# New costs and a new table of rank shifts in the planner of a fused recurrent-attention and gated-MLP kernel

## The chip, the core and the metric

The kernel runs on one core of a Trainium2 chip. The metric is the device time of one execution in microseconds (us); lower is better. TensorE (PE) multiplies matrices, VectorE (DVE), ScalarE (ACT) and GpSimd (POOL) do elementwise work, SyncE (SP) issues most DMA transfers. Every engine takes its own instructions strictly in program order, so an instruction that waits holds back all those behind it on its engine.

## The reference

Batch B is 4, heads H 8, sequence S 768, head dimension D 48; the model width is 384 and the inner width 1024. First a linear-attention recurrence runs over time for each batch and head, then a position-wise network with a short convolution in its gate:

```
for t in range(S):
    cur = u * k[t] (outer) v[t]
    y[t] = r[t] @ (state + cur)
    state = w[t][:, None] * state + k[t] (outer) v[t]
x = y, heads side by side                       # (4, 768, 384)
h = relu(x @ w_in)                              # 384 -> 1024
conv = sum over j of conv_w[j] * h shifted by j - 1 in time
out = (h * sigmoid(conv)) @ w_out               # 1024 -> 384
```

The weights arrive as 64-bit floats.

## The kernel before

The recurrence is cut into 24 chunks of 128 time steps, six to a batch (chunk n here; the stages in the planner are l, a and b). For each chunk: stage l loads w, k, r and v (line 602, four transfers of 192 KB each, small pieces); stage a transposes them on PE (637, after a small copy on ACT, 631), scans the decays on DVE (646, 654), multiplies (652, 658), transposes the keys back (705, copied out by ACT at 707 and 708), forms a diagonal on POOL (684, 686, 697) and sends a few rows to other partitions with six transfers (680, tile `last`); stage b does the score, state and output products on PE (846, 856, 878, 888) and writes x as a high and a low part (ACT 938, DVE 940), with six more transfers `xT<-xT` (949) after the fourth and the sixth chunk of a batch. The first four chunks have a longer form of stage b and no transfers of `last` (672 and 765 to 817). w, k and r have two buffers each, v three: chunk n + 2 can't be loaded before chunk n has released its buffer.

The network runs in 8 blocks of 384 time steps, two to a batch. A block is 8 units of nine matmuls of 386 columns each (960) into one PSUM bank, followed for each unit by the gate: ACT relu (972) and mul (973), two DVE steps (974, 976), ACT sigmoid (978), DVE product (979), ACT cast (981) and POOL difference (982), which makes the tile `gh`. Then 72 matmuls (989) per block multiply `gh` with w_out, three output tiles with 24 each, and ACT copies each out (1020) for SP to send (1021).

The weights are turned from 64-bit floats into a high and a low part during the first 70 us: three gathers of w_in issued by POOL (562), three transfers of w_out issued by SP (573), two of 1152 KB and one of 768 KB, and 17 pieces that go through ACT 513, DVE 515 and 518, POOL 521, ACT 535 and POOL 536. They share a ring of five large buffers with `gh`.

Which instruction comes when is decided by a planner at build time (class Plan). Each operation is recorded with an engine, a length from the table LEN, its dependencies, its buffers and a rank. `issue` then plays the engines forward with these lengths and always takes, of the operations that are ready on a free engine, the one with the lowest rank. The rank is the one the code gives plus two entries of the table SHIFT, one for the stage (a13, i2, l15 and so on) and one for the kind of operation in that sort of stage. The order that comes out is the program order of each engine; nothing is reordered on the chip. The places that matter:

```
def op(self, eng, us, f, r=(), w=(), holds=(), moves=0.0, port=False, rank=None):
...
        us = LEN[us] if isinstance(us, str) else us
...
        self.ops.append((eng, us, f, deps, bufs, moves, port,
                         (self.rank if rank is None else rank) + sum(SHIFT.get(x, 0) for x in self.tags[i]) + i * 1e-6))
```

Of the kernel before, what the change touches and what calls it, by code (L numbers as in the profile page):

```python
# [36 lines left out]

LEN = dict(
    tr=0.245, kback=0.245, scores=1.0, carried=0.794, state=0.45, y=0.86, state_y=1.22, mm3=0.529,
    cross=0.33, half=1.0, output=0.8, cph=0.35, sa=0.27, xhih=0.28, xloh=0.33,  # L40
    scan=0.86, small=0.1, pad=0.07, kt=0.47, dg=0.47, cp=0.62, xlo=0.6, sd=0.22, s=0.27,
    stt=0.54, gate=0.47, wts=0.47, wstt=0.47,
    fill=0.19, kh=0.37, guard=0.62, sbd=0.34, xhi=0.49, relu=0.41, mul=0.47, sig=0.43, cast=0.41, out=0.37, exp=0.46,
    z=0.98, zh=0.67, diag=1.07, lo=0.97,
    words=1.15, top=0.1, sdl=0.27, fetch=1.5, gather=1.6, rest=0.3, carried_rows=1.4, y_rows=1.5, ones=0.8,
    load=0.55, issue=0.45, spread=0.64,
)
SHAPE = dict(cross=3, half=3, output=3, scores=1, state=2, y=2, state_y=2, y_rows=2)
TURN = dict(tr=0.18, kback=0.18, carried=0.18)
PAUSE = 0.08  # L50
SHIFT = dict(
    a0=-1896, a1=-1164, a10=286, a11=83, a12=-1897, a13=911, a14=35, a15=-171, a16=-838, a17=1023, a18=300, a19=955,
    a2=-817, a20=586, a21=-198, a22=-206, a23=274, a3=1466, a4=-3102, a5=-229, a6=-1026, a7=10, a8=212, a9=-563,
    adg=1282, adiag=276, afill=1499, agather=13, aguard=-7, akback=213, akh=813, akt=-868, aones=389, apad=-30,
    ascan=-787, asmall=-226, aspread=-2165, atop=477, atr=208, az=393, azh=62, b1=1079, b10=-169, b12=280, b13=120,
    b15=457, b16=28, b17=396, b18=-3, b19=-2, b2=2308, b20=-53, b21=-561, b22=-32, b24=13, b3=1200, b4=735, b5=2,
    b6=-84, b7=-77, b8=111, b9=-911, bcarried_rows=234, bcp=20, bcph=432, bcross=-1208, bfill=93, bhalf=162, bkh=-259,
    boutput=-276, brest=97, bs=-396, bsa=-6, bscores=-136, bsd=-3, bsdl=-159, bsmall=-4, bspread=-44, bstate=56,
    bxhih=-258, bxloh=-167, by_rows=933, c=78, cexp=1328, cfill=595, cissue=24, clo=526, ctr=-113, cwords=-477,
    cwstt=94, cwts=43, i0=-1329, i1=-383, i2=266, i3=74, i4=-98, i7=-238, icast=-264, imm3=926, imul=12, irelu=-1875,  # L60
    isig=721, istt=-303, k=-7, kissue=22, ksmall=-75, l0=-32, l10=-37, l11=-2104, l12=3, l13=-294, l14=300, l15=702,
    l16=-1411, l17=589, l18=-103, l19=-154, l20=-57, l21=-30, l22=54, l23=-124, l3=-48, l4=95, l5=357, l6=82, l7=225,
    l8=668, l9=-175, lload=14, o0=-546, o1=-325, o2=210, o3=240, o4=-602, o6=60, o7=92, oissue=-254, omm3=1526,
    oout=-16, p0=-96, p1=-579, p10=77, p11=-444, p12=-378, p14=174, p15=52, p16=103, p2=-959, p3=-916, p4=17, p5=124,
    p6=357, p7=-445, p8=-626, p9=241, pcast=14, pexp=155, plo=-119, pwstt=100, pwts=107, q0=-465, q1=-346, q2=379,
    q3=-62, q4=91, q5=614, qissue=-23, qwords=31, w2=-1, w3=534, w5=112, w6=-73, wfetch=34, wissue=584,
)
TAIL = dict(PE=0.22, DVE=0.11, ACT=0.13, POOL=0.07, SP=2.3, LOAD=1.8)
BEGIN = dict(PE=4.3, DVE=3.0, ACT=3.2, POOL=8.3, SP=0.8)
# [1108 lines left out]
```

## Time and profile before

| what | value |
| --- | --- |
| median of 3 runs | 345.59 us (345.53, 345.59, 347.17) |
| the profiled execution | 346.11 us |
| its span, first to last instruction | 344.5 us |
| PE busy | 324.0 us, 94% of the span |
| DVE, ACT, POOL busy | 257.5, 228.4, 184.7 us |
| granted TensorE clock over the span | 0.98 |

The span is what the trace shows; 1.6 us of the profiled execution lie around it. A busy PE is not a PE at its peak, since matmuls overlap, and a granted clock under 1.00 in a stretch means that part of it ran at the lower of TensorE's two levels (1.2 GHz where 2.4 GHz is full).

### The profile page before, as it was taken

What the parts mean: (1) busy time and instruction counts of PE and PEld (TensorE: products, weight loads), DVE (VectorE), ACT (ScalarE), POOL (GpSimd) and SP (SyncE); (2) the same over time, 40 slices, a digit from 0 to 9 for tenths busy, and PEclk for the clock granted to TensorE, in tenths of its full rate; (3) what the DMA queues carried; (4) which work ended last, traced back from release to release, by engine and by line L of the source; (5) the groups of instructions that cost most, each with busy time, mean ns of one, the idle gap of its engine ahead of it and who ended that gap; (6) DMA issues with size and microseconds to landing.
All of it is one profiled execution on the core that took longest, in us unless ns stands there. A gap on an engine that the chain in (4) does not pass through costs nothing.

```text
span 344.5 us, 11004 instructions
## 1 busy us (share of the span) xinstructions
PE 324.0 (94%) x4278; PEld 302.1 (88%) x4278; DVE 257.5 (75%) x600; ACT 228.4 (66%) x610; POOL 184.7 (54%) x243
## 2 busy tenths in 40 slices
PE   8888886999999999899999999999999999999993
PEld 3877875889999989798999999999998999999992
DVE  4797999999999997679898788979575546786000
ACT  4276786897767652765868577565778998887201
POOL 8987999997376671244863185238122324444200
PEclk9989899999999999899999999999999999999998
DMA  8999945443456556366434533455747720000102
GB/s 155 278 307 324 231 94 102 90 80 79 85 122 134 105 119 129 71 139 122 107 65 108 123 84 69 94 107 126 242 133 211 233 66 25 24 0 26 50 23 73
DMA packets 114177, 40.95 MB, mean 119 GB/s; under 512 B 103021, under 2 KB 110726, under 8 KB 113350
## 3 DMA queue, kind: packets, MB, share of 16 engines
q1 hardware_dynamic: 112180, 30.74, 40.0%
q10 hardware_dynamic: 1506, 6.29, 5.9%
q0 software_dynamic: 432, 3.15, 2.2%
q8 instruction: 35, 0.57, 0.7%
q14 instruction: 24, 0.20, 0.2%
HBM read 31.48 MB, written 4.72 MB: 105 GB/s over the span
## 4 chain that ended last, share of the span: by engine, by line
PE 53%; POOL 11%; DMA 11%; DVE 8%; ACT 6%; SPq 5%; issue 4%; DVEq 0%; POOLq 0%; ACTq 0%
PE bank L989 21%; PE bank L960 20%; SPq L680 4%; PE bank L637 3%; DMA v<-in_v_dram 3%; DMA r<-in_r_dram 3%; POOL wide L521 2%; PE bank L846 2%; DMA gh<-in_moe_w_in_dram,limits 2%; DVE a L974 2%; PE bank L856 2%; POOL pm L697 2%; DVE g L979 1%; DVE a L976 1%; PE bank L878 1%
## 5 line engine op out<-in xcount | busy, mean ns | idle before, releaser
L989 PE MATMUL bank<-wo,gh 128*128 128x384 f32 x576 | 117.7, 346 | 0.8 <-POOL gh L982 0.6
L982 POOL TENSOR_TENSOR gh<-g,gh 128x384 fp32r<-128x384 f32 x64 | 64.5, 1016 | 93.0 <-ACT gh L981 90.0
L960 PE MATMUL bank<-xT,wi 128*128 128x386 f32 x576 | 112.4, 343 | 0.4 <-ACT xT L817 0.4
L960 PEld LDWEIGHTS bank<-xT,wi 128*128 128x128 f32 x576 | 101.1, 189 | 1.7 <-ACT xT L817 0.7
L989 PEld LDWEIGHTS bank<-wo,gh 128*128 128x128 f32 x576 | 100.1, 189 | 2.3 <-POOL gh L982 1.4
L974 DVE SCALAR_TENSOR_TENSOR a<-bank,cw,a 128x384 f32<-128x384 f32 x64 | 39.0, 612 | 21.3 <-ACT a L973 20.8
L979 DVE TENSOR_TENSOR g<-bank,a 128x384 f32<-128x384 f32 x64 | 34.9, 550 | 16.9 <-ACT a L978 12.4
L978 ACT ACTIVATE a<-a 128x384 f32<-128x384 f32 x64 | 33.3, 523 | 12.2 <-DVE a L976 12.2
L972 ACT ACTIVATE bank<-bank 128x386 f32<-128x386 f32 x64 | 30.6, 478 | 16.1 <-PE bank L960 15.8
L976 DVE SCALAR_TENSOR_TENSOR a<-bank,cw,a 128x384 f32<-128x384 f32 x64 | 39.0, 612 | 1.2 <-DVE a L974 0.5
L697 POOL TENSOR_SCALAR_AFFINE_SELECT pm<-dg 64x512 f32<-64x512 f32 x40 | 26.2, 655 | 22.8 <-PE bank L856 17.9
L973 ACT ACTIVATE a<-bank,cw 128x384 f32<-128x384 f32 x64 | 36.8, 578 | 0.4
L981 ACT CAST gh<-g 128x384 fp32r<-128x384 f32 x64 | 31.7, 509 | 7.9 <-DVE g L979 6.5
L684 POOL TENSOR_TENSOR z<-r,k 128x384 f32<-128x384 f32 x24 | 24.3, 1011 | 18.6 <-DVE dg L687 6.8
L646 DVE TENSOR_TENSOR_SCAN kr<-bank,one_end 128x387 f32<-128x387 f32 x24 | 22.9, 956 | 7.8 <-POOL kr L473 4.0
L686 POOL TENSOR_TENSOR z<-z,ubc 128x384 f32<-128x384 f32 x24 | 24.3, 1012 | 0.9
L1020 ACT COPY wide<-bank 128x384 f32<-128x384 f32 x24 | 11.4, 475 | 19.3 <-PE bank L989 19.2
L654 DVE TENSOR_TENSOR_SCAN kr<-bank,dA 128x387 f32<-128x387 f32 x24 | 22.9, 954 | 0.1
L846 PE MATMUL bank<-kr,sa 48*64 48x64 f32 (+1 forms) x240 | 17.4, 230 | 1.0 <-DVE bank L903 0.9
L846 PEld LDWEIGHTS bank<-kr,sa 48*64 48x64 f32 (+1 forms) x240 | 11.9, 126 | 6.3 <-issue 2.8
L521 POOL TENSOR_TENSOR wide<-wide,wide 128x384 int32<-128x384 int32 (+2 forms) x18 | 16.6, 932 | 1.3 <-DVE wide L518 1.1
L916 DVE COPY_PREDICATED pm<-upper_half,bank 128x256 f32<-128x256 int32 x40 | 17.1, 445 | 0.0
(133 smaller groups left out, 570.6 us busy)
## 6 DMA issues: line engine op xcount, KB each, us to landing
w<-in_w_dram SPq DMA_DIRECT2D x24, 192.0 KB, 3.6
k<-in_k_dram SPq DMA_DIRECT2D x24, 192.0 KB, 3.4
r<-in_r_dram SPq DMA_DIRECT2D x24, 192.0 KB, 3.5
v<-in_v_dram SPq DMA_DIRECT2D x24, 192.0 KB, 3.5
out_dram<-wide SPq DMA_DIRECT2D x24, 192.0 KB, 2.0
gh<-in_moe_w_in_dram ACTq DMA_DIRECT2D x3, 1024.0 KB
gh<-in_moe_w_out_dram SPq DMA_DIRECT2D x2, 1152.0 KB, 8.4
gh<-in_moe_w_out_dram ACTq DMA_DIRECT2D x2, 1152.0 KB, 6.2
```

The lines of the kernel that those rows point to most:

```text
L697: op("POOL", "zh", lambda p=slice(HL * j, HL * (j + 1)): nc.gpsimd.affine_select(out=halves(pm.t)[p].rearrange("p g m t -> p (g m) t"), in ...
L846: nc.tensor.matmul(to(h, m, c, w), lhsT=q["sa" if h else "sd"].t[p, m, 0:w], rhs=rt(out_of, m)[p, HL * h:HL * (h + 1)], start=first(h, c), ...
L960: nc.tensor.matmul(t.t[:, 0:HB + 2], lhsT=wi[:, m, a, f * P:(f + 1) * P], rhs=xT[:, x0 + m, c, xs], start=(m == 0 and j == 0), stop=(m == ...
L972: ("ACT", "relu", lambda: nc.scalar.activation(out=h(0, width + 2), in_=h(0, width + 2), func=AF.Relu), [t], [t]),
L973: ("ACT", "mul", lambda: nc.scalar.mul(out=a(), in_=h(1), mul=cw[:, 1, bass.ds(f, 1)]), [t, "cw"], [a1]),
L974: ("DVE", "stt", lambda: nc.vector.scalar_tensor_tensor(out=a(), in0=h(0), scalar=cw[:, 0, bass.ds(f, 1)], in1=a(), op0=ALU.mult, op1=ALU. ...
L976: ("DVE", "stt", lambda: nc.vector.scalar_tensor_tensor(out=a(), in0=h(2), scalar=cw[:, 2, bass.ds(f, 1)], in1=a(), op0=ALU.mult, op1=ALU. ...
L978: ("ACT", "sig", lambda: nc.scalar.activation(out=a(), in_=a(), func=AF.Sigmoid), [], [a1]),
L979: ("DVE", "gate", lambda: nc.vector.tensor_tensor(out=g.t[:, 0:width], in0=h(1), in1=a(), op=ALU.mult), [t, a1], [g]),
L981: ("ACT", "cast", lambda: nc.scalar.copy(out=part(0)[:, 0:width], in_=g.t[:, 0:width]), [g], [key]),
L982: ("POOL", "lo", lambda: nc.gpsimd.tensor_tensor(out=part(1)[:, 0:width], in0=g.t[:, 0:width], in1=part(0)[:, 0:width].bitcast(F32), op=AL ...
L989: nc.tensor.matmul(acc.t[:, 0:DM], lhsT=part(a)[:, tt * P:(tt + 1) * P], rhs=wo[:, f, c, :], start=(f == 0 and a + c == 0), stop=(f == FT ...
```

## The change

The operations, their lengths on the chip, their buffers and their dependencies are the same. Seventeen entries of LEN take other values, and every entry of SHIFT is replaced, so `issue` arrives at another order on every engine.

```diff
-    cross=0.33, half=1.0, output=0.8, cph=0.35, sa=0.27, xhih=0.28, xloh=0.33,
-    scan=0.86, small=0.1, pad=0.07, kt=0.47, dg=0.47, cp=0.62, xlo=0.6, sd=0.22, s=0.27,
+    cross=0.33, half=1.0, output=0.8, cph=0.35, sa=0.27, xhih=0.25, xloh=0.33,
+    scan=0.89, small=0.11, pad=0.07, kt=0.47, dg=0.47, cp=0.62, xlo=0.6, sd=0.33, s=0.27,
...
-    load=0.55, issue=0.45, spread=0.64,
+    load=0.78, issue=0.55, spread=0.73,
...
-    a0=-1896, a1=-1164, a10=286, a11=83, a12=-1897, a13=911, a14=35, a15=-171, a16=-838, a17=1023, a18=300, a19=955,
+    a0=-2057, a1=-2194, a10=-13, a11=-71, a12=-376, a13=3209, a15=146, a16=1883, a17=1338, a18=-258, a19=312,
...
```

All line numbers of the changed kernel are one higher, since the new SHIFT takes one line more. Three places of the order follow.

**SP at the start, from chunk 2's w.** `w_140` and `w_141` are the two buffers of w, and so on; `gh<-in_moe_w_out_dram` is a transfer of w_out. Before:

```order
L602 DMA w_140<-in_w_dram 128x8x48
L602 DMA k_142<-in_k_dram 128x8x48
L602 DMA r_144<-in_r_dram 128x8x48
L602 DMA w_141<-in_w_dram 128x8x48
L602 DMA k_143<-in_k_dram 128x8x48
L602 DMA r_145<-in_r_dram 128x8x48
L602 DMA v_146<-in_v_dram 128x8x48
L543 DMA wide_137<-in_moe_conv_w_dram 24x256
L573 DMA gh<-in_moe_w_out_dram 128x3x768 x2
L602 DMA k_142<-in_k_dram 128x8x48
L602 DMA r_144<-in_r_dram 128x8x48
L602 DMA w_140<-in_w_dram 128x8x48
```

With the change:

```order
L603 DMA r_144<-in_r_dram 128x8x48
L574 DMA gh<-in_moe_w_out_dram 128x3x768
L603 DMA w_141<-in_w_dram 128x8x48
L603 DMA k_143<-in_k_dram 128x8x48
L603 DMA r_145<-in_r_dram 128x8x48
L603 DMA v_146<-in_v_dram 128x8x48
L544 DMA wide_139<-in_moe_conv_w_dram 24x256
L603 DMA w_140<-in_w_dram 128x8x48
L603 DMA k_142<-in_k_dram 128x8x48
L603 DMA r_144<-in_r_dram 128x8x48
L603 DMA v_147<-in_v_dram 128x8x48
L574 DMA gh<-in_moe_w_out_dram 128x3x768
```

One of the two large transfers of w_out has moved ahead of chunk 3's four loads, the other behind chunk 4's.

**SP around chunks 13 to 15.** `last_161` are the rows of chunk 13, `last_162` those of chunk 14; `w_141`, `k_143` and `r_145` are the loads of chunk 15, `xT<-xT` the transfers of chunk 11's x. Before:

```order
L602 DMA k_143<-in_k_dram 128x8x48
L602 DMA w_141<-in_w_dram 128x8x48
L1021 DMA out_dram<-wide_137 128x384
L680 DMA last_161<-kr_155 16x2x130 x3
L602 DMA k_142<-in_k_dram 128x8x48
L680 DMA last_161<-kr_155 16x2x130 x3
L602 DMA w_140<-in_w_dram 128x8x48
L949 DMA xT<-xT 16x2x256
L680 DMA last_162<-kr_156 16x2x130 x6
L949 DMA xT<-xT 16x2x256 x5
L602 DMA v_148<-in_v_dram 128x8x48
L602 DMA r_145<-in_r_dram 128x8x48
```

With the change:

```order
L603 DMA w_141<-in_w_dram 128x8x48
L681 DMA last_161<-kr_155 16x2x130 x4
L681 DMA last_162<-kr_156 16x2x130 x6
L681 DMA last_161<-kr_155 16x2x130 x2
L603 DMA k_143<-in_k_dram 128x8x48
L603 DMA r_145<-in_r_dram 128x8x48
L1022 DMA out_dram<-wide_139 128x384
L1022 DMA out_dram<-wide_136 128x384
L603 DMA w_140<-in_w_dram 128x8x48
L603 DMA k_142<-in_k_dram 128x8x48
L603 DMA r_144<-in_r_dram 128x8x48
L950 DMA xT<-xT 16x2x256
```

Chunk 15's r has moved ahead of all `xT<-xT` transfers, and chunk 14's rows follow chunk 13's with no transfer of another kind between them.

**ACT between the key copies of chunks 13 and 14.** `kh_178` is chunk 13's copy, `kh_177` chunk 14's; `k_143` and `w_141` are the small copies in chunk 15's loads, `k_142` and `r_144` those in chunk 14's (before the change these stand further up). Before:

```order
L707 COPY kh_178<-bank_71 128x336
L708 COPY kh_178<-bank_71 128x2x48
L631 COPY k_143<-k_143 128x2x3x16
L631 COPY w_141<-w_141 128x2x3x16
L712 ACTIVATE junk,flags<-w_140,limits 128x384
L972 ACTIVATE bank_70<-bank_70 128x386
L707 COPY kh_177<-bank_69 128x336
```

With the change:

```order
L708 COPY kh_178<-bank_68 128x336
L709 COPY kh_178<-bank_68 128x2x48
L1021 COPY wide_136<-bank_69 128x384
L632 COPY k_142<-k_142 128x2x3x16
L632 COPY r_144<-r_144 128x2x3x16
L973 ACTIVATE bank_70<-bank_70 128x386
L713 ACTIVATE junk,flags<-w_140,limits 128x384
L708 COPY kh_177<-bank_69 128x336
L974 ACTIVATE a_190<-bank_70,cw 128x384
L709 COPY kh_177<-bank_69 128x2x48
L632 COPY w_141<-w_141 128x2x3x16
```

Block 2's first relu and chunk 14's key copy no longer stand behind the copies of chunk 15; chunk 15's k comes 18 rows after the last row shown.

## Rows read from the trace of the kernel before

**Rows 1.** Stretches: us, busy us by engine (x instructions), granted clock, DMA share, GB/s.
```profile
20.00:30.00 10.00, 8.61 (x79) 7.82 (x79) 8.01 (x18) 8.06 (x32) 9.28 (x11) 0.83 0.97 306
30.00:40.00 10.00, 7.98 (x83) 6.93 (x80) 9.81 (x23) 6.67 (x25) 8.28 (x11) 0.86 1.05 250
40.00:55.30 15.30, 12.60 (x193) 10.70 (x192) 14.88 (x35) 12.70 (x42) 15.05 (x17) 0.98 0.61 140
55.30:75.00 19.70, 17.45 (x330) 15.18 (x329) 18.91 (x44) 15.84 (x42) 19.40 (x23) 1.00 0.46 91
138.00:158.00 20.00, 17.63 (x310) 16.20 (x309) 14.84 (x37) 13.48 (x38) 6.37 (x7) 0.91 0.55 114
```

**Rows 2.** PE in order of time, 27 to 56 us: start, us, what, [idle before].
```profile
29.04 0.49 PE L637 MATMUL bank<-ident,w 128*128 128x128 f32 x3
...
34.46 0.55 PE L637 MATMUL bank<-ident,k 128*128 128x128 f32 x3 [1.03 <-ACT k L631]
...
36.59 0.55 PE L637 MATMUL bank<-ident,w 128*128 128x128 f32 x3 [0.99 <-ACT w L631]
...
55.27 0.33 PE L960 MATMUL bank<-xT,wi 128*128 128x386 f32 x1
```

**Rows 3.** SP in order of time, 9 to 38 us.
```profile
24.29 1.26 SPq L573 DMA_DIRECT2D gh<-in_moe_w_out_dram  x2
25.72 0.37 SPq L602 DMA_DIRECT2D k<-in_k_dram  x1
```

**Rows 4.** DMA queues, 14 to 17 us: packets, MB, share of 16 engines; then transfers.
```profile
q0 software_dynamic: 159, 1.20, 98.9%
q1 hardware_dynamic: 118, 0.02, 3.6%
...
w<-in_w_dram SPq DMA_DIRECT2D x1, 192.0 KB, 9.2
```

**Rows 5.** DMA packets by size, 0 to 50 us.
```profile
DMA packets 29484, 11.72 MB, mean 234 GB/s; under 512 B 27853, under 2 KB 28070, under 8 KB 29094
```

**Rows 6.** SP in order of time, 126 to 158 us.
```profile
132.55 0.51 SPq L602 DMA_DIRECT2D k<-in_k_dram  x1
...
145.02 4.30 SPq L949 DMA_DIRECT2D xT<-xT  x5
```

**Rows 7.** ACT in order of time, 128 to 150 us.
```profile
135.85 0.27 ACT L631 COPY k<-k 128x96 f32<-128x96 f32 x1 [3.56 <-DMA k<-in_k_dram]
```

**Rows 8.** PE in order of time, 136 to 158 us.
```profile
135.75 3.34 PE L960 MATMUL bank<-xT,wi 128*128 128x386 f32 x18
...
141.19 0.28 PE L878 MATMUL bank<-last 48*64 48x64 f32 x3 [0.74 <-DMA last<-kr]
...
142.91 0.27 PE L846 MATMUL bank<-kr,sa 48*48 48x64 f32 x2 [0.92 <-DVE bank L903]
```

**Rows 9.** The chain of work that ended last, 126 to 158 us: start, us, what.
```profile
149.99 3.31 DMA r<-in_r_dram
```

**Rows 10.** The page's costliest groups: busy us, mean ns of one, idle before.
```profile
L982 POOL TENSOR_TENSOR gh<-g,gh 128x384 fp32r<-128x384 f32 x64 | 64.5, 1016 | 93.0 <-ACT gh L981 90.0
...
L974 DVE SCALAR_TENSOR_TENSOR a<-bank,cw,a 128x384 f32<-128x384 f32 x64 | 39.0, 612 | 21.3 <-ACT a L973 20.8
L979 DVE TENSOR_TENSOR g<-bank,a 128x384 f32<-128x384 f32 x64 | 34.9, 550 | 16.9 <-ACT a L978 12.4
L978 ACT ACTIVATE a<-a 128x384 f32<-128x384 f32 x64 | 33.3, 523 | 12.2 <-DVE a L976 12.2
L972 ACT ACTIVATE bank<-bank 128x386 f32<-128x386 f32 x64 | 30.6, 478 | 16.1 <-PE bank L960 15.8
L976 DVE SCALAR_TENSOR_TENSOR a<-bank,cw,a 128x384 f32<-128x384 f32 x64 | 39.0, 612 | 1.2 <-DVE a L974 0.5
...
L973 ACT ACTIVATE a<-bank,cw 128x384 f32<-128x384 f32 x64 | 36.8, 578 | 0.4
L981 ACT CAST gh<-g 128x384 fp32r<-128x384 f32 x64 | 31.7, 509 | 7.9 <-DVE g L979 6.5
```

More of the change, by code (lines that the diff above doesn't have):

```diff
@@ L39 @@
     tr=0.245, kback=0.245, scores=1.0, carried=0.794, state=0.45, y=0.86, state_y=1.22, mm3=0.529,
-    cross=0.33, half=1.0, output=0.8, cph=0.35, sa=0.27, xhih=0.28, xloh=0.33,
-    scan=0.86, small=0.1, pad=0.07, kt=0.47, dg=0.47, cp=0.62, xlo=0.6, sd=0.22, s=0.27,
[L42 to L45, printed above, removed]
-    load=0.55, issue=0.45, spread=0.64,
+    cross=0.33, half=1.0, output=0.8, cph=0.35, sa=0.27, xhih=0.25, xloh=0.33,
+    scan=0.89, small=0.11, pad=0.07, kt=0.47, dg=0.47, cp=0.62, xlo=0.6, sd=0.33, s=0.27,
+    stt=0.55, gate=0.48, wts=0.47, wstt=0.47,
+    fill=0.17, kh=0.335, guard=0.62, sbd=0.34, xhi=0.49, relu=0.5, mul=0.47, sig=0.43, cast=0.41, out=0.36, exp=0.46,
+    z=1.03, zh=0.73, diag=1.07, lo=0.97,
+    words=1.28, top=0.1, sdl=0.27, fetch=1.1, gather=1.6, rest=0.3, carried_rows=1.4, y_rows=1.5, ones=0.8,
+    load=0.78, issue=0.55, spread=0.73,
 )
@@ L51 @@
 SHIFT = dict(
-    a0=-1896, a1=-1164, a10=286, a11=83, a12=-1897, a13=911, a14=35, a15=-171, a16=-838, a17=1023, a18=300, a19=955,
[L53 to L66, printed above, removed]
+    a0=-2057, a1=-2194, a10=-13, a11=-71, a12=-376, a13=3209, a15=146, a16=1883, a17=1338, a18=-258, a19=312,
@@ new lines @@
+    a2=-1084, a20=1326, a21=89, a22=434, a23=308, a3=1309, a4=289, a5=-565, a6=-247, a7=392, a8=1512, a9=330,
+    adg=1873, adiag=142, afill=983, agather=259, aguard=-135, akback=143, akh=-1, akt=-1628, aones=-50, apad=-1864,
+    ascan=-1570, asmall=-1284, aspread=-2790, atop=-202, atr=475, az=1186, azh=-12, b0=-150, b1=-205, b10=433,
+    b11=138, b12=2839, b13=-24, b14=438, b15=231, b16=915, b17=2524, b18=338, b19=579, b2=4688, b20=1384, b21=1569,
+    b22=27, b23=308, b24=-15, b3=-200, b4=-271, b5=-582, b6=-128, b7=-116, b8=236, b9=-114, bcarried_rows=709, bcp=21,
@@ new lines @@
+    bcph=1659, bcross=-488, bhalf=-1629, bkh=1054, boutput=-211, brest=-51, bs=-2437, bsa=203, bscores=119, bsd=-794,
+    bsdl=207, bsmall=-10, bspread=-1361, bstate=-63, bxhih=-122, bxloh=-466, by_rows=-250, c=176, cfill=651,
+    cissue=-41, clo=-25, ctr=37, cwords=40, cwstt=-58, cwts=-288, i0=-1775, i1=-478, i2=-584, i3=113, i4=48, i5=29,
+    i6=32, icast=-343, igate=-129, ilo=-12, imm3=1565, imul=679, irelu=-413, isig=-105, istt=-660, k=-129,
+    kissue=-743, ksmall=52, l1=-4, l10=238, l11=-329, l12=-48, l13=40, l15=238, l16=722, l17=349, l18=-1442, l19=-31,
@@ new lines @@
+    l2=9, l20=-216, l21=-789, l22=144, l23=-378, l3=-259, l4=-1, l5=-227, l6=44, l7=215, l8=-100, l9=-251, lload=313,
+    o0=-538, o1=1042, o2=-329, o3=77, o4=16, o5=39, o6=15, oissue=-353, omm3=4953, oout=-467, p0=271, p1=-17, p10=352,
+    p11=553, p12=5, p13=881, p14=931, p15=-674, p2=-82, p3=-12, p4=839, p5=-481, p6=-163, p7=1574, p8=256, p9=-89,
+    pcast=-1281, pexp=-563, plo=-3754, pwstt=-743, pwts=-250, q0=-1082, q1=-284, q2=144, q3=3, q4=20, q5=-220,
+    qissue=8, qwords=-244, w2=-195, w3=-27, w4=-9, w5=206, w6=472, wfetch=-331, wissue=4699,
```

## The prediction

> **What bounds the kernel now.** I read the stretches first, since the busy share of the whole span mixes stages with different limits. PE's end is the kernel's end, so what can be won is time in which PE idles or runs at its lower clock. In [rows 1] each stretch gives the length, then PE's busy time, and further right the granted clock. From 20 to 55.3 us PE is idle for 1.39 + 2.02 + 2.70 = 6.1 us, and the clock of 0.83, 0.86 and 0.98 says that 0.17 x 10 + 0.14 x 10 + 0.02 x 15.3 = 3.4 us of full-speed work were not granted. In the same rows DMA is busy to 0.97 and 1.05 until 40 us, and POOL and DVE are busy for 15.05 and 14.88 of the 15.3 us that follow: PE waits for data first and for the conversion of the weights and chunk work second. From 55.3 to 75 us PE is idle for 2.25 us while POOL is busy for 19.40 of 19.70 us and DVE for 18.91: a stage bound by these two, with PE fed as they deliver. From 138 to 158 us PE is idle again, for 2.37 us, with a clock of 0.91, which is another 0.09 x 20 = 1.8 us, and here no engine is full: DVE 14.84 of 20, ACT 13.48, POOL 6.37. That is a knot of waits, not a bound.
>
> Then I looked up who ends these waits. In the head, PE's two longest single waits between 20 and 40 us are for ACT's small copies in chunk 4's loads, 1.03 and 0.99 us [rows 2]; these loads stand on SP right behind both large transfers of w_out, issued from 24.29 us on [rows 3]. In the knot, the order on ACT makes it wait 3.56 us for chunk 15's k [rows 7], which SP issued only at 132.55 us [rows 6]; block 2's relu and chunk 14's key copy stand behind that copy. PE then waits 0.74 us for the last transfers of chunk 13's rows and 0.92 us on DVE [rows 8], the clock falls, and chunk 15's r, issued at 149.99 us behind the `xT<-xT` copies that end at 149.3 [rows 6], takes 3.31 us to arrive and stands on the chain that ended last [rows 9].
>
> **The change part by part.** No instruction is removed or added; all the price is in the order.
>
> *The head.* One transfer of w_out, 1152 KB, moves ahead of chunk 3's loads, the other behind chunk 4's. From 14 to 17 us the engines moved 1.20 + 0.02 MB in 3 us [rows 4], 0.40 MB per us, so one such transfer fills them for about 2.9 us (1.18 MB). Gain: chunk 4's loads have one transfer less in front of them, up to 2.9 us; the waits that the trace puts down to them are 1.03 + 0.99 us, so I take 2.0. Price: chunk 3's loads have one more in front of them, up to 2.9 us. What hides it is that the first of them is issued at 14.44 us [rows 3] and takes 9.2 us to land [rows 4], so until 23.6 us, and PE turns chunk 3 only at 29.04 us [rows 2]: 5 us of cover. Gone, the cover costs the full 2.9. A second price is that the moved transfer now shares the engines with the gathers of w_in, which feed the first conversions on all three of ACT, DVE and POOL. The only row for sharing is [rows 4]: SP's queue, with chunk 3's loads in it, got 3.6% beside the gathers' 98.9%. Bounds: 0 (it is starved as those loads were) to 2.9 us (it goes first). I take 1.0, nearer to the row. Head: -2.0 + 1.0 = -1.0 us, between -2.9 and +3.9 (2.9 for the gathers, 1.0 for chunk 3 beyond its cover).
>
> The Trainium skill, "DMA: Bandwidth & Descriptors", section "Queues, rings and completion order", says that a DMA engine goes round its queue rows and drains a whole packet of one before it turns to the next. That speaks against this part of the change: packets of the gathers had 1.20 MB / 159 = 7.5 KB [rows 4], those of w_out 3.07 MB / 1024 = 3.0 KB (the 1024 packets between 2 and 8 KB) [rows 5], so w_out would not be starved like the small loads but take 29%; the first gather (1.05 MB) would need 3.7 us in place of 2.6, a price of 1.1 where I have 1.0, and the sum would be 0.1 us higher. The 98.9% beside 3.6% for packets of about 0.2 KB agrees with it.
>
> *55.3 to 75 us.* By the trace's lengths POOL has 4.6 us less work ahead of its first `gh`, but DVE has 68.8 us ahead of the output product of chunk 5, where it had 68.1. A stretch in which DVE is 96% busy is not shortened by that: 0, at best -2.25 (all of PE's idle time).
>
> *The knot.* In the new order chunk 15's k and r stand on SP ahead of the `xT<-xT` copies and of two outputs, and on ACT chunk 15's k stands behind most of block 2's gates, so nothing queues behind the wait of 3.56 us. By the trace's lengths, the new order has 16.3 us of PE work between chunk 13's last transposes and its scores where the old one has 13.4, for chunk 14 22.9 in place of 15.3, and chunk 15's k and r are issued some 8 us of PE work ahead of their transposes. Queued behind a late `last` transfer there is now nothing of chunk 15 that PE needs soon. The knot holds 2.37 + 1.8 = 4.2 us. I take 1.0 of it as staying, since chunk 14's rows now split chunk 13's in two and PE needs the last two: -3.2, between 0 (it moves elsewhere) and -4.2.
>
> *Shorter covers.* The new order does chunks later and network blocks closer together. One unit's gate, by [rows 10], takes 0.478 + 0.578 + 2 x 0.612 + 0.523 + 0.550 + 0.509 + 1.016 = 4.9 us from the matmuls' end to `gh`, when nothing else stands in the queues. I counted in both orders the PE work between a unit's last matmul and the first that reads its `gh`, at 0.177 us a matmul (18 in 3.34 us, less the last one's 0.33) [rows 8]: the median over 64 units falls from 25 to 15 us, the smallest from 6.3 to 5.2, and units under 8.5 us rise from 5 to 7. What hides the gate there is just that work; where other steps stand between on ACT, DVE or POOL, PE waits. Two more tight units at 0.4 us, half of the 0.7 to 1.0 us that single waits of PE take [rows 2, 8], give +0.8; bounds 0 and +3 (each of the seven waits 0.4 us).
>
> Sum: -1.0 + 0 - 3.2 + 0.8 = -3.4 us. Against the profiled execution, 346.11 us (span 344.5 and 1.6 around it), that is 342.7. That execution is 0.52 us above the median of the three runs, so against the median: **342.2 us**.
>
> **The rivals.**
> *The knot moves.* The loads, rows and copies share one SP queue, and work that no longer blocks chunk 15 blocks another chunk; chunk 13's rows being split is a candidate, and so is block 3, which now waits for the last `xT<-xT` copy behind chunk 15's rows. For it: nothing in the change makes a transfer shorter. Against it: the work between chunk 13's to 23's transposes and scores has a median of 13.7 us where it was 11.0, and no chunk has less than 10.5 (it was 8.8). With -1.0 for the head, 0 for the knot and +0.8: 345.4.
> *Gates too late.* The seven tight units cost 3.0 in place of 0.8: 344.4.
> *More comes free.* If DVE is fed sooner in the head, all that is bound by it until 75 us starts sooner, and the clock isn't lowered again; head -2.9, knot -4.2, covers +0.8: 339.3; with no cost of covers 338.5.
> *SP is late from the start.* The mechanism that ends on the other side: the w_out transfer ahead of chunk 3 delays the gathers and chunk 3's loads, and SP, which issues in order, is behind from there on: +3.9 for the head, no gain at the knot, since chunk 15's loads then come as late as they did. 345.6 + 3.9 = 349.5. For it: the DMA engines are 97% to 105% busy from 20 to 40 us [rows 1], so nothing catches up before that. Against it: the 5 us of cover. It decides if the first matmul of block 0 starts later than 55.27 us [rows 2] by 2 us or more.
> The Trainium skill's rule on packets only adds to that last rival: by it the gathers lose 1.1 us, which alone leaves the forecast's sign as it is.
>
> **How the numbers follow.** Forecast 0.50, more comes free 0.10, gates too late 0.10, the knot moves 0.17, SP late 0.13. The three runs lie within 0.5% of each other, so 0.5%, 1.73 us, is about what can be told from no change: faster means under 343.9, slower over 347.3. The forecast and the freer case are faster, 0.60; the two at 344.4 and 345.4 are the same, 0.27; the last is slower, 0.13. The range reaches from 338.8 (nearly all of both pots) to 346.8, which leaves out most of the slower rival and a little of the freest case. The forecast's own range is 340.2 to 343.9.
>
> **What would show it.** Right: no wait of ACT over 1 us for a k load between 125 and 160 us, PE busy for all but 1 us of that knot and a clock of 1.00 there; no wait of PE on chunk 4's copies, and block 0's first matmul at 53 to 55 us. Wrong: that matmul after 57 us; the first gather's conversion starting later than 19 us; a new wait on `last`, `xT` or a load over 1 us anywhere between 75 and 262 us; waits of PE on `gh` (989 on POOL 982) adding up to more than 2 us. The prediction is wrong above all if the knot was the symptom of a full SP queue, which would then show up at another chunk at the same price.

## The result: slower, against a forecast of 1%

The changed kernel takes 349.21 us (median of 20 runs, 345.05 to 351.48), the kernel before 345.65 us (median of 20, 344.64 to 347.99). The ratio is 1.0061 with a 95% interval of 1.0034 to 1.0089; it leaves out the runs over 1.5% above the fastest, four of the 20 here, and the medians lie further apart (1.0103) because six runs of the changed kernel took 345.05 to 346.99 us and fourteen 348.55 to 351.48, for a reason that stays open. The forecast was 342.2 us. The profiled execution of the changed kernel took 351.0 us (span 349.2), 1.8 us above its median.

The stretches of the changed kernel, with the columns of [rows 1]:

```profile
20.00:30.00 10.00, 7.74 (x70) 6.48 (x71) 7.26 (x17) 6.73 (x26) 8.27 (x9) 0.83 0.92 272
30.00:40.00 10.00, 9.62 (x108) 8.59 (x104) 6.77 (x19) 7.41 (x30) 6.54 (x7) 1.00 0.97 243
40.00:55.30 15.30, 11.96 (x178) 10.19 (x178) 14.38 (x34) 9.95 (x34) 12.30 (x15) 0.89 0.62 143
55.30:75.00 19.70, 15.22 (x196) 12.93 (x193) 18.89 (x43) 15.97 (x44) 18.61 (x21) 0.91 0.33 67
138.00:158.00 20.00, 20.00 (x315) 19.34 (x307) 15.95 (x38) 14.38 (x39) 10.04 (x12) 1.00 0.62 132
270.00:280.00 10.00, 5.93 (x161) 5.01 (x159) 3.79 (x11) 4.64 (x10) 3.52 (x5) 1.00 0.87 230
280.00:290.00 10.00, 10.00 (x91) 9.61 (x91) 2.80 (x7) 6.01 (x12) 0.00 (x0) 0.83 0.56 189
```

Three things are to be seen. The knot of 138 to 158 us is gone: PE is busy for 20.00 us at a clock of 1.00. From 40 to 75 us PE is busy for 27.2 us where it was 30.1, at a clock of 0.89 and 0.91 where it was 0.98 and 1.00 [rows 1]. And there is a hole that the kernel before does not have: 4.07 us of idle PE at 270 to 280 us, with 1.7 us (0.17 x 10) of clock lost behind it.

The same stretch in the kernel before:

```profile
270.00:280.00 10.00, 10.00 (x58) 10.00 (x58) 6.12 (x12) 8.68 (x20) 4.03 (x4) 1.00 0.73 231
```

PE of the changed kernel in order of time, at six places (columns as in [rows 2]):

```profile
24.80 0.90 PE L638 MATMUL bank<-ident,w 128*128 128x128 f32 x3 [1.44 <-ACT w L632]
...
40.58 0.52 PE L638 MATMUL bank<-ident,r 128*128 128x128 f32 x3 [0.65 <-ACT r L632]
...
44.29 0.55 PE L638 MATMUL bank<-ident,w 128*128 128x128 f32 x3 [2.29 <-ACT w L632]
...
57.83 0.34 PE L961 MATMUL bank<-xT,wi 128*128 128x386 f32 x1
...
273.59 0.51 PE L879 MATMUL bank<-kr 48*64 48x64 f32 x19 [1.39 <-issue]
...
279.71 0.21 PE L847 MATMUL bank<-last,sa 48*48 48x64 f32 x1 [2.67 <-issue]
```

Block 0 starts at 57.83 us, 2.56 us later than before [rows 2]. The two waits of 1.39 and 2.67 us stand in the middle of the products of stages b23 and b24 (the last of the stages b; "chunk 24" in the expectations is b24, which only completes chunk 23), among matmuls of the same group, and nothing in the trace released them: "issue" is time in which the engine waited for nothing that the profile shows. They are not peculiar to this execution: the profiled executions of e1, e5, e12, e13 and e14 below have two such waits at the same products, 2.7 to 4.6 us together, and e5's is the shortest of its twelve runs.

To see where time goes I also gave each kind of PE step one length for all kernels (0.33 us for a transposition, 0.53 us for three gate or output matmuls, and so on), summed these lengths over the PE steps in the kernel's own order, and took the sum from the start that the trace shows. This lag grows wherever PE waits or runs at the lower clock. It comes from one execution of each kernel. In us:

```
PE work ahead                      10    25    30    60    90   130   220   250   300
before                           13.6  22.8  26.0  30.0  29.6  35.3  35.3  36.6  36.7
changed                          16.5  25.6  28.9  35.1  35.8  35.7  34.9  41.5  41.7
changed, no re-reads (e3)        16.0  27.3  30.6  36.5  37.2  37.0  37.1  37.5  37.7
old head, new rest (e5)          14.3  23.0  26.4  30.5  31.3  31.2  30.6  34.2  34.5
chunk 2's rows first (e13)       12.9  21.6  25.5  31.7  32.3  32.2  31.5  38.6  38.8
```

Block 0 begins at 30 us of work. So the change loses some 3 us until then and 2 more until 60; where the old order loses 5.7 between 90 and 130 (the knot) the new one loses nothing; and between 220 and 250 it loses 6.6 us at one place.

### The profile page after: what moved, and what is told of

Read it like the earlier page. It is cut to its first block, busy times and chain, and to the rows that moved or that the text cites. A ratio compares the mean times of both kernels' runs of the same rounds, so it can differ in the third digit from the quotient of the medians.

```text
span 349.2 us, 11000 instructions
## 1 busy us (share of the span) xinstructions
PE 323.0 (92%) x4278; PEld 301.9 (86%) x4278; DVE 258.1 (74%) x600; ACT 229.5 (66%) x610; POOL 185.0 (53%) x243
## 4 chain that ended last, share of the span: by engine, by line
PE 77%; DVE 7%; POOL 4%; issue 3%; ACT 3%; DMA 3%; DVEq 0%; POOLq 0%; ACTq 0%
PE bank L990 29%; PE bank L961 28%; PE bank L638 5%; PE bank L847 4%; PE bank L857 3%; PE bank L879 3%; DMA gh<-in_moe_w_in_dram,limits 3%; PE bank L889 2%; PE bank L706 2%; DVE kr L647 1%; POOL wide L522 1%; DVE bank L516 1%; DVE wide L519 1%; DVE kr L653 1%; DVE sd L733 1%
## 5 line engine op out<-in xcount | busy, mean ns | idle before, releaser
L961 PE MATMUL bank<-xT,wi 128*128 128x386 f32 x576 | 114.8, 346 | 2.2 <-DVE kr L653 0.9
L982 ACT CAST gh<-g 128x384 fp32r<-128x384 f32 x64 | 32.4, 511 | 11.6 <-DVE g L980 10.1
L939 ACT CAST xT<-bank 112x256 fp32r<-112x256 f32 x40 | 13.5, 379 | 14.5 <-PE bank L857 14.5
L638 PE MATMUL bank<-ident,w 128*128 128x128 f32 x72 | 13.0, 291 | 6.6 <-ACT w L632 3.7
```

Of the source, the lines that this page charges most:

```text
L638: nc.tensor.transpose(out=cols(m), in_=src.t[:, 2 * m:2 * m + 2, :].rearrange("p h d -> p (h d)"), identity=ident)
L961: nc.tensor.matmul(t.t[:, 0:HB + 2], lhsT=wi[:, m, a, f * P:(f + 1) * P], rhs=xT[:, x0 + m, c, xs], start=(m == 0 and j == 0), stop=(m == ...
L982: ("ACT", "cast", lambda: nc.scalar.copy(out=part(0)[:, 0:width], in_=g.t[:, 0:width]), [g], [key]),
```

## The experiments

Every time is the median of the runs made (6 for e1 and for e10, e11, e12, e14 and e17, 5 for e16, else 12); "R" is the ratio to the kernel before, taken as in the section above against runs made beside them, with its 95% interval. The kernel before had medians of 345.67 to 346.38 us there. The changed kernel has R 1.0061, and 0.001 of R is 0.35 us. Line numbers differ from kernel to kernel by the lines that the edit adds ahead. `place`, `MOVES` and `target` act on the finished order: a row is taken out and put ahead of another row of its engine.

**e1, the w_out transfer put back behind chunk 4's loads.**

```diff
+MOVES = [(('w4', 'issue', 0), ('w5', 'issue', 0))]
...
+        for a, b in MOVES:
+            j = place(*a)
+            x = order.pop(j)
+            order.insert(place(*b), x)
```

> The changed kernel with one issue of SP moved: the w_out transfer that stands ahead of chunk 3's loads goes behind chunk 4's, beside the other one; no other row of any engine moves. Theory H (the moved transfer is what the head lost: it shares the DMA engines with the gathers of w_in and holds chunk 3's loads back): the first conversion starts at 17.5 us again in place of 19.3, chunk 3's first transposes come some 3 us earlier, block 0's first matmul at 54 to 56 us in place of 57.8, and the time falls from 349.2 to 344 to 346 us. Rival R (the head lost because the new order puts the conversions of the weights later on ACT, DVE and POOL, behind chunk work): block 0's first matmul stays within 1 us of 57.8, and the time at 348 to 350 us.

Measured: 350.0 us, R 1.0118 [1.0073, 1.0163]; no gain. The first conversion did start earlier (18.1 us), but both transfers now stand ahead of chunk 5's k, which takes 8.99 us to land and is on the chain that ends at block 0 (start, us, what):

```profile
31.97 8.99 DMA k<-in_k_dram
40.97 0.02 issue
40.99 0.27 ACT k L641
```

**e2, the same transfer moved forward in the kernel before.** The edit is `MOVES = [(('w4', 'issue', 0), ('l3', 'load', 0))]`.

> The kernel before with one issue of SP moved, the converse of the experiment above: the first w_out transfer goes ahead of chunk 3's loads, where the change has it. Theory H: block 0's first matmul moves from 55.3 to 57.5 us or later and the time rises from 345.6 to 348 to 350 us. Rival R: the cover that I counted on holds, block 0 starts at 55 to 56 us, and the time is 345 to 346.5 us.

Measured: 346.33 us, R 1.0005 [0.9974, 1.0037]. Block 0 started at 57.3 us, and the time did not follow. With e1 this takes theory H away: the transfer is not what the head lost.

**e3 and e4, without the second readings of the weights.** These are six transfers that ACT issues near the end, with two scans each; the scans are ACT's, not DVE's as the expectation has it.

```diff
+LEFT_OUT = ('q0', 'q1', 'q2', 'q3', 'q4', 'q5')
...
+        order[:] = [x for x in order if self.tags[x[1]][0] not in LEFT_OUT]
```

> The changed kernel without the six second readings of the weights near the end and their twelve scans on DVE (part of the range check of the weights is left out). Theory T (at 272 to 280 us PE waits for its own instructions, whose 16 KB fetches share the DMA engines with these readings while three chunks' state products, short matmuls, stand close together): no idle time of PE over 0.5 us put down to 'issue' between 265 and 285 us, a clock of 1.00 there, and 349.2 less 1.4, 2.7 and about 1.7 of clock, 343.5 to 345.5 us. Rival U (these waits are data that the trace doesn't name, or chance): two waits of over 1 us stay at chunks 23 and 24's products, and the time is 348 to 350 us.

> The kernel before without the same six readings and twelve scans, the control for the run above. Theory T: nothing stalls PE's supply in this order, where the stages with short matmuls are spread over longer stretches, so the time is 345.6 less 0 to 0.7 us. Rival V (the readings cost every order alike, by DMA share or by DVE's time): it falls by the same 3 to 5 us as the changed kernel does.

Measured: the changed kernel falls to 344.27 us, R 0.9943 [0.9920, 0.9967], 4.9 us less; the kernel before to 345.73 us, R 0.9993 [0.9964, 1.0022], nothing measurable. In e3 the hole is gone, and the lower clock behind it:

```profile
270.00:280.00 10.00, 10.00 (x329) 8.95 (x320) 6.02 (x19) 4.37 (x13) 4.32 (x5) 1.00 0.32 66
280.00:290.00 10.00, 10.00 (x59) 10.00 (x58) 3.31 (x8) 3.58 (x8) 0.00 (x0) 1.00 0.14 41
```

The DMA queues between 257 and 271 us (packets, MB, share of 16 engines), first the changed kernel, then e3:

```profile
q10 hardware_dynamic: 286, 2.10, 45.5%
q1 hardware_dynamic: 1542, 0.60, 16.4%
```

```profile
q1 hardware_dynamic: 1473, 0.50, 14.5%
q8 instruction: 2, 0.03, 1.2%
```

Without the readings (q10) the 16 engines are busy for 16% of this stretch in place of 62%. The queue of kind "instruction" moves packets of 16 KB; I take it to carry PE's own instructions, for the reason given below. Two of its packets fall into these 14 us in e3, while the changed kernel's stand just outside them, at 256.4 and 271.2 us: nearly 15 us apart where they are 12 in e3. The packets one by one, from the trace's DMA records:

```
start us, us, PE rows executed since the packet before
changed  256.4 0.93 331 | 271.2 0.93 412 | 276.5 1.69 271 | 282.2 1.06 137
e3       258.6 1.35 336 | 270.5 1.25 270 | 274.8 0.92 276 | 278.4 1.34 202
before   252.0 0.93 276 | 263.9 1.12 470 | 267.5 1.83  40 | 288.3 1.45 239
```

PE has some 250 rows a packet on average (8,675 rows, 35 packets). In e3 the one for b23 comes 270 rows after the one before it, in the changed kernel 412, and PE stops 1.0 us after its start (at 272.2). It stops again at 277.0 us, 0.5 us after the start of the next. Both times it runs again 1.4 to 1.5 us after the packet has landed. So it is in all six executions with such waits (the changed kernel, e1, e5, e12, e13, e14): each of the twelve waits ends 1.3 to 1.7 us after a packet of this queue has landed, and that is the reason for taking the packets for PE's instructions. A long stretch of rows does not make a wait by itself: the kernel before has a packet that is later still (470), but there the short products are over and three matmuls take 0.53 us.

**e5, the first 56 us of every engine in the old order, the rest in the new one.** The planner plays both sets of tables (`old`, `new`), and a third pass issues each engine's rows in the order of a given list.

```diff
+        for e in target:
+            head = [i for at, i in old if at < 56.0 and self.ops[i][0] == e]
+            target[e] = head + [i for i in target[e] if i not in set(head)]
+        order = self.play(now, target)
```

> Every engine's rows of the first 56 us in the order of the kernel before, all later rows in the order of the change. Theory S (the head's 5 to 6 us are lost by the order of the rows there as a whole, chunk 2's copies behind the first conversions and a wait of DVE for chunk 3's z, and what follows is as good as the trace shows it): block 0's first matmul at 55 to 56.5 us, the stretch 120 to 262 us without idle time of PE as in the change, the stall at chunks 23 and 24 kept; 349.2 less 3 to 5.5, so 343.7 to 346.2 us. Rival W (the two halves belong together: the later order leans on where the head left chunks and loads, or 55 to 120 us is bound by DVE and POOL whatever the head gives): the gain is given back in new waits between 56 and 120 us, and the time is 347 to 350 us.

Measured: 346.03 us, R 0.9996 [0.9971, 1.0022], 3.2 us under the changed kernel. The knot does not come back and the hole stays, with two waits on "issue" of 1.4 and 1.3 us:

```profile
138.00:158.00 20.00, 20.00 (x222) 19.42 (x221) 16.56 (x36) 15.96 (x42) 12.33 (x14) 1.00 0.55 123
262.00:280.00 18.00, 15.30 (x371) 13.73 (x371) 7.69 (x22) 12.29 (x26) 5.53 (x7) 1.00 0.77 240
```

**e6, e7, e9, e15: the readings moved instead of left out.** In e6 the last four go behind chunk 24's products; e7 is e6 with the old head.

```diff
+        MOVES = (
+            (('q2', 'issue', 0), ('b24', 'xhih', 0)),
+            (('q3', 'issue', 0), ('b24', 'xhih', 0)),
+            (('q2', 'words', 0), ('q4', 'words', 0)),
...
+            (('q4', 'words', 0), ('i6', 'relu', 4)),
...
+            (('q5', 'words', 0), ('i6', 'sig', 6)),
...
+            (('k', 'small', 2), ('i7', 'mm3', 15)),
```

> The changed kernel with the last four second readings of the weights moved on ACT behind chunk 24's products (the readings' eight scans, which are ACT's, and the three small steps that use their flags move back with them); nothing is left out. Theory T (PE's instruction fetches share the DMA engines with the readings while short matmuls use up instructions fast): the two waits on 'issue' of 1.4 and 2.7 us and the half-clock stretch behind them are gone as in the run without the readings, and the time is 344.5 to 346.5 us, that run's 344.3 plus up to 2 us for eight scans among block 6's and 7's gates. Rival X (it was not the fetch but the scans' place on ACT or the readings' sum of bytes): the time stays at 348 to 350 us.

> Both edits together: the first 56 us in the order of the kernel before, the rest in that of the change, with the last four readings behind chunk 24's products. If the head's loss and the stall at the end are separate and the knot's gain stays, the two gains add up: 349.2 less 3 to 5.5 and less 3 to 4.5, so 339.5 to 343 us, which beats both kernels. If one of them hides the other, it is no better than the better of the two single edits.

Measured: 347.30 us, R 1.0022 [0.9993, 1.0051], and 346.17 us, R 0.9990 [0.9958, 1.0023]. The waits on "issue" are gone at the end in both (e7 has one of 0.4 us, at 35.8 us), but others have come. PE's waits of e7 (engine, line, waited for: us in total, times, longest):

```profile
PE bank L1044 <- DMA xT<-xT: 2.0, 1, 2.0
PE bank L1223 <- DVE fsum L1221: 1.6, 1, 1.6
```

The readings now share the DMA engines with the transfers of chunk 24's x, and a small product waits for the flags of the late scans. e9 sets the readings behind block 6's first matmuls and that product later; e15 moves each reading by one slot only.

```diff
+            (('q2', 'issue', 0), ('i6', 'mul', 0)),     # e9
+            (('q3', 'issue', 0), ('i6', 'relu', 1)),
...
+            (('k', 'small', 2), ('o7', 'mm3', 3)),
...
+            (('q2', 'issue', 0), ('q4', 'issue', 0)),   # e15
...
+            (('q3', 'issue', 0), ('q5', 'issue', 0)),
...
+            (('q4', 'issue', 0), ('q3', 'words', 0)),
```

> As the run with both edits, with the four late readings issued only when block 6's first matmuls have begun, and the small steps on their flags set later: in that run PE waited 2.0 us for the transfers of chunk 24's x, which now shared the DMA engines with the readings, and 1.6 us on the sum of the flags, two waits that the edit itself had made. Theory (head, knot and stall are separate terms): both waits gone, no wait on 'issue' over 0.5 us, and the time 346.2 less 3 to 4.5, 341 to 343.5 us, faster than either kernel. Rival (the readings cost some 3 us wherever they stand behind chunk 22): a wait of the same size elsewhere among blocks 6 and 7, and 345 to 346.5 us.

> The splice of the old first 56 us with the new rest, with the second readings 2 to 5 each moved back by one slot on ACT: the third starts behind chunk 23's products, the fourth with block 6, so that only one more pair of scans falls among block 6's gates than in the change, and none among block 7's. Theory T with a price for the scans (the readings starve PE's instruction fetch at chunks 23 and 24, and scans among the gates cost PE up to 3 us as in the two runs with all four moved): no wait on 'issue' over 0.5 us, a rise of PE's lag behind chunk 22 of 0.5 to 1.5 us, and the time 342.5 to 344.5 us. Rival (readings cost 2 to 3 us wherever they stand): 345 to 346.5 us.

Measured: 345.25 us, R 0.9980 [0.9952, 1.0008], and 346.25 us, R 1.0009 [0.9976, 1.0042]. e15 waits for `xT` again (2.3 us). In e9 the two waits that e7 had made are gone, but ACT is busier where the late scans stand among block 6's gates (17.08 and 18.05 of 20 us, 16.49 and 15.87 in e5), PE idles there for 0.74 + 0.57 us, 1.1 us of it for `gh`, and does 106 and 107 matmuls where e5 does 115 and 115; its lag grows by 3.0 us:

```profile
280.00:300.00 20.00, 19.26 (x106) 18.30 (x106) 8.84 (x16) 17.08 (x33) 3.96 (x4) 1.00 0.64 222
300.00:320.00 20.00, 19.43 (x107) 18.50 (x106) 15.28 (x28) 18.05 (x42) 7.00 (x7) 1.00 0.00 1
```

**e10, the splice without the readings** (e5's edit and e3's).

> The splice (first 56 us in the order before, the rest in the new one) without the six second readings and their scans (part of the range check of the weights is left out): the bound for the run above. If the terms add, 346.0 less the 3.8 us that PE's lag grew by behind chunk 23 in the splice, 341 to 343 us; if the head's gain and the stall are one and the same lost time, 344 us, as the changed kernel without the readings.

Measured: 342.82 us, R 0.9875 [0.9823, 0.9927]. By R the head and the stall add: 0.0065 (the changed kernel less e5) and 0.0118 (the changed kernel less e3) make 0.0183, and e10 is 0.0186 below the changed kernel. By the medians they don't quite: 3.2 and 4.9 us, but 6.4 together; e10's six runs reach from 340.31 to 346.10 us. So moving the readings cost most of what leaving them out saves, which the rivals of e9 and e15 had said.

**e11, the converse splice**: `new` gives the first 56 us, `old` the rest.

> The converse splice: the first 56 us in the new order, all later rows in the order before. If head, knot and stall are separate: the knot is there (PE idle for over 1.5 us between 120 and 165 us), no wait on 'issue' at the end, and the time is 346 plus the 3.2 us that the splice took away, 348 to 350.5 us. Rival (the new head suits only its own rest, or a head that is late is made up for where DVE and POOL are the bound): 345.5 to 347 us.

Measured: 352.20 us, R 1.0161 [1.0112, 1.0210]. The knot is there, with the clock down again:

```profile
138.00:158.00 20.00, 18.17 (x189) 16.50 (x190) 13.39 (x35) 9.80 (x29) 4.64 (x6) 0.83 0.40 82
```

That is 1.7 us more than the theory's range. e16 and e17 below show that a seam can cost by itself, so I take from e11 only that the knot belongs to the old order behind 56 us.

**e8 and e12, single suspects of the head.** The chain of the changed kernel that leads to block 0 passes a wait of DVE for chunk 3's z, with the pieces 3 to 8 of the weights behind it (columns as in [rows 2]):

```profile
33.98 0.55 DVE L688 TENSOR_REDUCE dg<-z 128x8 f32<-128x384 f32 x1 [3.12 <-POOL z L687]
```

e8 puts that wait into the old order; e12 gives the pieces their old ranks in the new one.

```diff
+        MOVES = (                                     # e8, on the order before
+            (('a3', 'dg', 0), ('c', 'wstt', 0)),
+            (('c', 'lo', 0), ('p3', 'lo', 0)),
+        )
...
+OLD = SHIFT_0                                         # e12
+LEN_0, SHIFT_0 = LEN, {**SHIFT, **{x: OLD.get(x, 0) for x in (*SHIFT, *OLD) if x[0] == "p"}}
```

> The kernel before with the order of the change at one place of the head: on DVE chunk 3's sum over z stands right behind the first step of the conv weights, ahead of their second step and chunk 3's scans, and on POOL the conv weights' low part stands behind chunk 3's diagonal. Theory D (this wait of DVE is a main part of the head's loss): DVE idles for some 2.3 us at 28.3 us, PE's turn of the conv weights and what stands behind it comes 1.5 to 2 us later, block 0's first matmul at 56.8 to 58 us, and the time rises to 347 to 348 us. Rival E (later slack takes it up; the loss is chunk 2's late transposes and the many small delays behind them): the time stays within 0.8 us of 345.7.

> The changed kernel with the shifts of the weights' 17 pieces alone (the entries that begin with p) as they were before, for the first 58 us; chunks 0 to 5 keep the new shifts, and all rows after 58 us the new order. On DVE the pieces 3, 5 and 8 stand 2, 5 and 8 rows earlier. Theory P (the head loses 1.4 us before block 0 and 2 us behind it, because pieces 3 to 8 stand behind chunks 4 and 5): PE's lag behind its own work at block 0's end falls from 34.9 us to 32 to 33.5, and the time from 349.2 to 346.5 to 348 us. Rival Q (it is chunk 2's and 3's copies behind the first pieces): no change, 348.5 to 350 us.

Measured: e8 347.04 us, R 1.0008 [0.9987, 1.0030], 0.7 above the kernel before beside it (346.38). PE did wait 3.6 us for the conv weights and block 0 started at 57.2 us, and most of it was made up, which is nearer to rival E. e12 351.56 us, R 1.0138 [1.0084, 1.0192]: no gain. Its pieces do start earlier, and a chunk's transposition now waits for ACT behind a piece's cast:

```profile
45.17 0.77 PE L701 MATMUL bank<-ident,w 128*128 128x128 f32 x3 [1.97 <-ACT wi L599]
```

**e13 and e14, chunk 2's rows moved forward in the changed kernel, and the conv weights besides.** There ACT's copy of chunk 2's w stood behind the casts of pieces 0 and 1, at 24.49 us.

```diff
+            (('a2', 'fill', 0), ('p0', 'exp', 0)),      # e13: 12 moves
+            (('a2', 'tr', 0), ('b0', 'rest', 0)),
...
+            (('a2', 'scan', 0), ('p2', 'wstt', 0)),
...
+            (('c', 'wstt', 0), ('a3', 'z', 1)),         # e14: 14 more
+            (('c', 'lo', 0), ('a3', 'z', 1)),
...
+            (('p3', 'wts', 0), ('a3', 'top', 0)),
```

> The changed kernel with chunk 2's rows alone moved forward to about where they stood before: on ACT its three small copies ahead of the first pieces of the weights, on PE its transposes ahead of chunk 0's and 1's later products, on DVE its scans and key products ahead of chunk 1's steps. Theory Q (chunk 2, late by 5 us behind the first pieces, is what the head loses): its first transposes at 20 to 22 us in place of 24.8, PE's lag at block 0's end 2 to 3 us lower, and the time from 349.2 to 346 to 347.5 us. Rival R2 (no single place: DVE and POOL owe the same work later anyway): within 1 us of 349.2.

> The run with chunk 2 moved forward, and besides the conv weights' conversion moved ahead of chunk 3's sum over z on DVE and ahead of chunk 3's second product on POOL, with pieces 3 and 4 of the weights directly behind it. Theory Q2 (chunk 2's delay and DVE's 3.1 us wait for z, behind which pieces 3 to 8 stand, are the head's loss together): pieces 3 to 5 start 2 to 4 us earlier, the 3.1 us wait shrinks below 1.5 us, and the time is 345.5 to 347 us. Rival R2: no more than the run with chunk 2 alone gains, or no gain at all.

Measured: e13 348.04 us, R 1.0050 [1.0012, 1.0087]; e14 350.91 us, R 1.0120 [1.0075, 1.0165]. Chunk 2's transposes came at 20.70 us in e13, and in its profiled execution the lag at 60 us of work fell to 31.7 (the table above), but the median gained 1.2 us and R 0.0011 (0.4 us), and its interval holds the changed kernel's almost wholly, so no gain is shown. In the same execution the hole at the end took 7.1 us, with waits on "issue" of 3.2 and 1.4 us.

**e16 and e17, old head, new middle, old end**, with the second seam at 222 or 198 us.

```diff
+            head = [i for at, i in old if at < 56.0 and self.ops[i][0] == e]
+            head += [i for at, i in new if at < 222.0 and self.ops[i][0] == e and i not in set(head)]
+            target[e] = head + [i for i in self.rows(old, e) if i not in set(head)]
```

> Three pieces: the first 56 us in the order before, then the new order up to 222 us, then the order before again for the rest, so that the second readings and chunks 22 to 24 stand as they stood before the change, and nothing is left out. If head, knot and stall are three separate places: the knot's gain stays (PE without idle time over 0.5 us between 120 and 200 us), no wait on 'issue' over 0.5 us at the end, and the time is the splice's 346.0 less 3 to 4, 342 to 343.5 us, faster than both kernels. Rival (the readings' price belongs to the new order's middle, which leaves the end fuller whoever orders it, or the seam at 222 us makes a wait of its own): 345 to 347 us.

> The same with the second seam at 198 us, which tells a wait at the seam from one of the pieces: if the pieces are separate it is within 1 us of the run with the seam at 222 us, and 342 to 344 us; if the seam decides, the two differ by more than 1.5 us.

Measured: 352.29 us, R 1.0199 [1.0172, 1.0225], and 351.86 us, R 1.0187 [1.0146, 1.0227]. Up to the seam both have PE busy for all of 120 to 200 us; there the lag of e17 jumps from 30.9 to 40.0, behind waits such as these:

```profile
203.89 0.27 PE L907 MATMUL bank<-kr,sa 48*64 48x64 f32 x1 [1.86 <-DVE xT L1001]
206.49 0.81 PE L939 MATMUL bank<-kr 48*64 48x64 f32 x19 [1.95 <-DVE kr L715]
```

The two agree within 0.5 us at a time that neither theory nor rival had: at either seam the lag jumps by some 9 us. I take it that the old end needs other steps done than the new middle has done; that is not shown beyond the waits above. They say nothing on the readings. No version that does all the work is shown to be faster than the kernel before; e9 comes nearest.

## Why the prediction was wrong

Two steps of the sum failed, the head and a term that was missing. With one of the two mended the time is inside the range of 338.8 to 346.8 us: 344.27 us without what made the missing term (e3), 346.03 us with the old head (e5).

**The head: the first step that failed.** "Head: -2.0 + 1.0 = -1.0 us" should have been +2.2 by R (the changed kernel less e5, 1.0061 and 0.9996) or +3.2 by the medians (349.2 less e5's 346.0). I costed what moved on SP, because rows of waits led there, and took the new order of ACT, DVE, POOL and PE in the first 56 us as free. The price of the transfer itself was well bounded: 0.2 us in e2 for a term of 1.0. The gain of 2.0 did not come. Between 15 and 60 us the small copies on ACT wait for no load any more (3.3 us in all before), so the loads are no longer what is late; but the copies now stand late in ACT's own order, and PE waits 1.44, 0.65 and 2.29 us for three of them (chunk 2's w, chunk 4's r and chunk 5's w), 4.4 us in all, where it was 1.03 + 0.99 [rows 2] and 0.46 us at 23.8 us. SP issued as forecast:

```profile
11.28 0.84 SPq L574 DMA_DIRECT2D gh<-in_moe_w_out_dram  x1
14.46 0.37 SPq L603 DMA_DIRECT2D w<-in_w_dram  x1
...
31.52 0.57 SPq L574 DMA_DIRECT2D gh<-in_moe_w_out_dram  x1
```

Between 14 and 17 us the DMA queues of the changed kernel show the sharing:

```profile
q0 software_dynamic: 106, 0.75, 64.4%
q1 hardware_dynamic: 219, 0.36, 33.0%
```

SP's queue (q1), with w_out in it, got 33.0% beside the gathers where the small loads had got 3.6% [rows 4], and the first conversion on DVE started at 19.3 us (17.5 before). The Trainium skill, "DMA: Bandwidth & Descriptors", section "Queues, rings and completion order", has engines go round the queue rows packet by packet, which gave 29%: the trace comes near with 33.0%, and e2's with 27.9%.

Where the head loses inside its 56 us is shown only in part. Over the nine kernels with the old head unedited the lag at 30 us of work is 27.7 on average and at 60 it is 32.1; over the four with the new one it is 29.6 and 35.5. So 1.9 us are lost before block 0 and 1.5 behind it, in the stretch where I had forecast 0 because DVE's work ahead of chunk 5 is the same sum. Equal sums did not help: DVE is busy for 28.4 us between 20 and 55.3 in the changed kernel where it was 32.7 [rows 1], so it owes more when block 0 starts. The same thirteen traces show when: counting PE's idle time and the clock that was not granted, PE loses 7.3 us from 20 to 40 us with the old head and 4.2 with the new, but 5.6 and 10.6 us from 40 to 65 us, where the granted clock is 0.95 on average with the old head and 0.81 with the new. So the new head gains 3.1 us in the first of these stretches and loses 5.0 in the second, over half of that by running at the lower clock. Chunk 2's rows account for 1.2 us at most as the medians have it, and by R for 0.4 (e13); which rows account for the rest stays open; splices inside the head were not tried.

**The knot: right.** "-3.2" measured -4.1 by R and -2.9 by the medians, as e10 stands to e4: both have the old head and no readings, and differ in the order behind 56 us, covers included (0.9875 and 0.9993; 342.82 and 345.73 us). ACT waits for no k load any more between 125 and 160 us; its longest waits there are for PE:

```profile
ACT bank L973 <- PE bank L961: 3.4, 4, 1.5
ACT wide L1021 <- PE bank L990: 2.8, 2, 2.3
```

And e5 and e11 show that the knot goes with the order behind 56 us, whichever head is ahead of it. The rival that it moves elsewhere fell: from 75 to 262 us the longest waits of PE are 0.8 and 0.6 us.

**Shorter covers: +0.8 measured 0.** No wait of PE on `gh` is left; ahead of all 576 matmuls of the output product it idles for 0.6 us, on ACT's copy of an output tile.

**The term that was missing, the second step that failed: the hole at 272 to 280 us,** +4.1 by R (1.0061 less e3's 0.9943) or +4.9 by the medians, for which the sum had nothing. The new order puts b22, b23 and b24, of 128, 128 and 64 short matmuls with as many weight loads, within 15 us, at the time when ACT's readings fill the DMA engines (0.87 in that row). In the old order the same readings cost 0.4 us (e4), which is not clear of noise. I had looked for new waits between 75 and 262 us, and only at data.

Sum, by R: 2.2 - 4.1 + 0 + 4.1 = 2.2 us, against 2.1 for the ratio of 1.0061. By the medians it is 3.2 - 2.9 + 0 + 4.9 = 5.2 against 3.6, so a term taken from medians is good to some 2 us only. In each of the three pairs the intervals of R don't overlap, so that the signs are clear of noise; but they reach 0.2% to 0.5% to either side, 0.8 to 1.8 us, and no size here is known better than that.

The rival "SP is late from the start" gave 349.5, the right time for a reason that did not hold: the knot's gain did come. Its test, block 0 later by 2 us, came true (57.83) and was a poor one, since e2 and e8 started block 0 nearly as late (57.3 and 57.2) and lost 0.2 and 0.7 us. Here a start that slipped in front of a stretch bound by DVE and POOL was not a loss yet; the lag behind that stretch was.

## What to carry to other kernels

An order that a planner finds anew must be costed on every engine and over the whole span. Where the diff shows SP's rows best, the loss may sit on ACT and DVE; compare how much work each engine has done at a few times, not only who waits. Look also at what no dependency shows: a dense group of short instructions beside large transfers waited here with no releaser in the profile, most likely for its instructions. And a seam between two good orders can cost more than either saves (e16, e17), so parts of an order are not exchanged like parts of code.

## What the runs showed of the hardware

Packets of kind "instruction" come by DMA during the run, through the same engines as the data, and those of one queue are most likely PE's instructions: 35 of 16 KB in the changed kernel:

```profile
q8 instruction: 35, 0.57, 0.7%
```

A packet took 0.88 to 1.55 us, and 1.69 us at 276.5 us beside the readings. That the readings make the waits is shown by e3 and e10 (no readings: at most 0.5 us on "issue") and by e6 and e9 (readings elsewhere: none). That a late packet is what PE waits for rests on the times, twelve waits that end 1.3 to 1.7 us after a landing; how far ahead PE's instructions are asked for was not measured. Behind the hole the granted clock of the changed kernel was 0.83 from 280 to 290 us, although PE was busy throughout; in e5, with a smaller hole, it stayed at 1.00.

Single runs of one order lie far apart: the changed kernel's from 345.05 to 351.48 us, and the lag at 60 us of work in nine kernels with the same old head from 30.0 to 35.6 us. One profiled execution is no measure of a term of 2 us.
